# Local and coarse attention and two MoE layers in float32: the first phase's steps in another order, with fewer alternations of TensorE's kinds of work

## The chip, the cores and the metric

The kernel runs on one core of a Trainium2 chip. The metric is the device time of one execution in microseconds (us), the median of several executions.

## The reference

```python
# q, k, v: (4, 8, 576, 64)
out_d     = softmax(q_d @ k_d.T / 8) @ v_d       # q_d, k_d, v_d: means of 4 neighbours, 144 rows
out_local = softmax(where(|i - j| < 4, q @ k.T / 8, -1e9)) @ v
x = repeat(out_d, 4) + out_local                 # -> (2304, 512)
h = max(x @ w1, x @ w2, x @ w3)                  # (2304, 768)
y = h @ w_out                                    # (2304, 512)
g = max(y @ w_in, 0)                             # (2304, 2048)
out = (g * g) @ w_out2                           # (2304, 512)
```

Attention inputs are float32. The weights come as 8-byte floats and are turned into float32 on the chip.

## The kernel before

**Two phases.** Phase 1 computes attention and the first MoE layer (`y`) batch by batch, and decodes the weights of both layers. Phase 2 computes the second layer in three blocks of 768 tokens; it is one long row of matrix products, and the change doesn't touch it. Every product of the two layers runs as three products of high and low parts (`mm3`, L188 to L191: hi*hi, hi*lo, lo*hi).

**Steps and tokens.** Phase 1 is a list of some 1,300 tokens in `CFG["phase1"]`. A loop (L933) reads it, `act_on` (L679) calls the function of each token, and `manual_schedule` keeps that order on every engine. Nothing is reordered afterwards: on each engine (and in SyncE's queue of DMA issues) the instructions stand exactly in the order of the tokens, each waiting for its own inputs. So the list is at once the order of TensorE, VectorE, ScalarE, GpSimd and SyncE. The digits of a token are its batch, head pair, tile and so on; `F` and `B` are the first 256 and the last 320 positions of a batch.

- Attention, `a..`: `al`, `am`, `aN` load q, k and v (SyncE). `aq`, `ak` pool q and k (VectorE in batch 0, GpSimd after). `as` scores (TensorE, L348 and L355), `aa` maxima (VectorE), `ae` exponentials (ScalarE), `ar` sums (VectorE), `au`, `av` norms (GpSimd in batch 0, VectorE after), `at`, `af`, `aT` transposes (TensorE, L423 and L433), `ay`, `az`, `aY` copies of them, `ao` products with v (TensorE, L473 and L482), `aX`, `ah`, `ad` the sum and its high and low part (`ad` is `x_lo`, VectorE L517).
- First layer: `gg` (and `gK` in four pieces) is a gate product, 12 matmuls of 256 or 320 columns; `gM` the maximum over three gates (VectorE L591, or a copy on ScalarE for the first), `gA`, `gB` its high and low part, `gG` the output product, 18 matmuls, `gZ` its copy and store.
- Weights of the first layer come in pairs of 1 MB: `wD` load, `wR` rebias (VectorE L172), `wL` low bits (ScalarE), `wJ`, `wI` two joins (VectorE L546), `wH` high part (ScalarE), `wS` low part (VectorE L562, GpSimd for the last three pairs). Three raw buffers (`stg`) serve them, so a load waits for the `wS` three pairs back. Second layer: `x..`, `y..`, `z..` in the same manner.
- `bN` issues N products of zeros (`keep_busy`, L644) on TensorE, two matmuls each, whose results nobody reads.

**What TensorE does in phase 1.** Gates, output products, transposes and dummies use all 128 rows and columns of the array. Scores use 64 by 64 quarters of it, and products with v 70 or 72 rows by 64 columns. These two kinds are called the small kinds below, the others the full kinds. All attention steps share four PSUM banks (a second-half scores step takes two), gates and outputs four others.

Of the kernel before, what the change touches and what calls it, by code (L numbers as in the profile page):

```python
# [59 lines left out]
wR6 gg0130 gM0031 aX10F gB011 ah10F wJ6 aN11F gg0032 gM0130 wD10 ad10F wI6 gg0131 wL8 gM0032 wH6 wR8 gg0050 gM0131  # L60
gA003 wS6 gg0132 gM0050 wJ8 wD11 wL10 gg0140 wR10 gB003 gM0132 gA013 wJ10 gg0040 gM0140 wI8 gg0141 gM0040 wI10 wH8
wR11 wL11 gg0041 gB013 gM0141 wH10 wS8 gg0142 wJ11 xD4f gg0042 gM0041 gM0142 wS10 gA014 gg0051 gM0042 gA004 as11F
gM0051 wI11 gg0052 am12 xL4f aa11F gB004 gg0150 gB014 wH11 gM0052 xR4f ae11F as11B wS11 gg0151 aa11B al13 gA005
gM0150 gB005 ar11F as12F ae11B xJ4f gG000 aa12F av11F ae12F aq13 ar11B gg0152 gM0151 av11B gZ000 au11B at11F au11F
ao10B ar12F ay11F ak13 aT11F gM0152 gG001 aN11B aU10B aw12 aY11F aX10B gA015 av12F ah10B xI4f ao11F ad10B gZ001
au12F xs4 at11B xa4 aN12F as12B aU11F ay11B gB015 xc4 gG002 al20 aa12B aX11F ae12B gG003 ya4 yc4 za4 gZ002 aT11B
af11B as13F ar12B aY11B au12B az11B av12B ah11F at12F gZ003 ao11B aa13F aq20 zc4 aT12F gG010 aU11B ay12F aY12F ae13F
ad11F ak20 aX11B ah11B ar13F ao12F aN12B ad11B gZ010 av13F at12B am13 au13F aU12F at13F aX12F af12B gG013 ay12B
aN13F ah12F az12B xD4o ay13F ad12F aw13 aT13F as13B gZ013 aY13F aT12B aa13B al21 gG012 aY12B ae13B xR4o am20 ao13F
gG011 aN20F gZ012 ar13B aq21 xL4o au13B av13B aU13F aX13F ao12B gZ011 xJ4o as20F ah13F aN13B aU12B ad13F at13B aa20F  # L70
ak21 af13B gg1000 az13B aw20 ay13B ae20F gg1030 aX12B xI4o aT13B ah12B ar20F gM1000 gg1001 xe4 ad12B av20F au20F
aY13B gg1031 xD5f gM1001 gM1030 ye4 ao13B gM1031 gg1032 aU13B aX13B ah13B ze4 gg1002 gM1032 ad13B gA103 gB103 as20B
gM1002 xL5f xR5f gg1050 gA100 aa20B aN20B am21 as21F gM1050 gB100 ae20B xJ5f at20F al22 gg1040 ay20F aa21F gg1051
gM1040 aw21 ar20B ae21F av20B aT20F gg1052 gM1051 au20B xI5f aY20F at20B ao20F aq22 gM1052 xa5 ay20B aT20B aN21F
ar21F af20B aU20F gg1041 gA105 ya5 aY20B az20B aX20F za5 gg1110 ah20F gB105 gM1041 ad20F av21F xs5 gg1042 gM1110
am22 au21F xc5 as21B gM1042 ak22 gA104 gg1100 aa21B al23 gB104 gg1111 ae21B yc5 zc5 gg1101 gM1111 gM1100 ar21B aq23
av21B gg1112 gM1101 au21B xD5o as22F ak23 gM1112 gA111 gg1120 aa22F gB111 ae22F gg1140 gM1120 gg1102 ar22F gM1140
av22F au22F xL5o xR5o at21F gM1102 gg1020 ay21F gA110 xJ5o aT21F gg1021 gM1020 aY21F gB110 xI5o as22B gM1021 xe5
gg1121 aa22B al30 ye5 gg1130 ae22B xD6f gM1121 gg1122 gM1130 ar22B aq30 av22B gg1131 gM1122 ze5 au22B gA112 gg1141
gB112 ak30 gM1131 xL6f xR6f gg1132 gM1141 xJ6f gg1142 gM1132 xI6f gA113 as23F gB113 xa6 gM1142 gg1022 xs6 gA114  # L80
ao21F gB114 xc6 gM1022 gg1150 aa23F aN22F gA102 aU21F aX21F ae23F gB102 at22F ya6 gg1151 ay22F za6 ah21F gM1150
ar23F ad21F aT22F au23F gg1152 gM1151 aY22F av23F yc6 as30F gM1152 xD6o ao20B gA115 aa30F gg1010 aU20B aw22 aX20B
ae30F gB115 at21B gG110 ay21B aN21B ah20B ar30F gM1010 zc6 av30F ad20B au30F xL6o xR6o af21B gg1011 az21B gZ110 xJ6o
aT21B gg1012 am23 gM1011 aY21B xI6o ao21B gM1012 xe6 ao22F aN22B aU21B gA101 ye6 at22B xD7f aU22F at23F gG112 aw23
ay22B aX22F ay23F ah22F gB101 ad22F gG111 aN23F gZ112 aX21B ze6 ah21B ad21B xL7f xR7f af22B gG102 gZ111 xJ7f az22B
am30 xI7f aT23F gG100 gZ102 xs7 xa7 aY23F ya7 xc7 aT22B gG103 za7 aY22B yc7 gZ100 ao22B gZ103 xD7o ao23F aU22B aw30
aX22B gG101 aU23F ah22B ad22B aX23F as23B gZ101 aN23B ah23F am31 gG113 aa23B al31 xL7o ad23F xR7o ae23B gg2000 xJ7o
aN30F zc7 xI7o as30B gM2000 gZ113 ar23B aq31 gg2010 aa30B xe7 gg2020 al32 gM2010 au23B ae30B av23B ye7 gg2011 ak31
ze7 gM2020 at23B ar30B gg2012 gM2011 ay23B au30B av30B af23B aT23B az23B aq32 gM2012 as31F aY23B gA201 xD0f as31B
# [1096 lines left out]
```

## Time and profile before

| what | us |
|---|---|
| median of 3 runs (lowest, highest) | 819.86 (817.78, 820.36) |
| the profiled execution's own time | 818.96 |
| its span, first to last instruction | 817.2 |
| TensorE busy | 805.1 |
| VectorE, ScalarE, GpSimd busy | 514.3, 321.3, 173.7 |

Phase 1 lasts until 433.23 us, where the first product of phase 2 starts. The difference of 1.8 us between span and time lies around the program. Matmuls are pipelined: one starts before the last one's end is drawn, so costs are read from start to start, not from the lengths.

### The profile page before, as it was taken

How to read it: one execution, taken by the hardware profiler on the slowest of the kernel's cores; microseconds unless marked ns; L12 is line 12 of the kernel's file. 1: busy time of each engine (PE TensorE's matmuls, PEld its weight loads, DVE VectorE, ACT ScalarE, POOL GpSimd, SP SyncE). 2: the span in 40 equal slices, each digit the busy share in tenths (PEclk: the TensorE clock that was granted, in tenths of full speed). 3: DMA queues.
4: the chain of work that ended last, by engine and by line, in shares of the span. 5: the costliest groups of instructions: out<-in, count | busy, mean ns of one | idle time of the engine just before them, and what ended most of it. 6: DMA issues, size and time to landing. Idle time of an engine off the chain costs nothing.

```text
span 817.2 us, 15421 instructions
## 1 busy us (share of the span) xinstructions
PE 805.1 (99%) x6130; PEld 748.2 (92%) x6130; DVE 514.3 (63%) x960; ACT 321.3 (39%) x893; POOL 173.7 (21%) x195
## 2 busy tenths in 40 slices
...
GB/s 291 262 99 199 162 112 241 190 147 166 158 254 303 208 8 8 78 102 23 252 389 252 144 276 191 0 1 102 310 118 190 1 1 54 256 141 164 31 1 77
DMA packets 60768, 121.84 MB, mean 149 GB/s; under 512 B 5304, under 2 KB 29464, under 8 KB 60696
## 3 DMA queue, kind: packets, MB, share of 16 engines
...
q8 instruction: 48, 0.79, 0.4%
q14 instruction: 24, 0.20, 0.1%
...
## 4 chain that ended last, share of the span: by engine, by line
PE 90%; DVE 6%; DMA 2%; ACT 0%; issue 0%; SPq 0%; ACTq 0%; DVEq 0%
PE g L189 10%; PE g L191 9%; PE g L190 9%; PE po L190 8%; PE po L189 8%; PE po L191 8%; PE P L189 7%; PE P L191 7%; PE P L190 7%; PE yp L189 3%; PE yp L190 3%; PE yp L191 3%; DMA raw_p<-in_wg 1%; DVE raw_p L546 1%; DMA v<-in_vP 1%; DMA out_y<-ob 0%
## 5 line engine op out<-in xcount | busy, mean ns | idle before, releaser
L189 PE MATMUL g<-xhi,hi_p 128*128 128x256 f32 (+1 forms) x576 | 174.9, 304 | 0.0
L191 PE MATMUL g<-xhi,lo_p 128*128 128x256 f32 (+1 forms) x576 | 170.3, 296 | 1.4 <-DVE lo_p L562 1.4
L190 PE MATMUL g<-xlo,hi_p 128*128 128x256 f32 (+1 forms) x576 | 169.8, 295 | 0.0
L191 PEld LDWEIGHTS g<-xhi,lo_p 128*128 128x128 f32 x576 | 108.2, 188 | 2.0 <-DVE lo_p L562 2.0
L189 PEld LDWEIGHTS g<-xhi,hi_p 128*128 128x128 f32 x576 | 108.3, 188 | 1.8
L190 PEld LDWEIGHTS g<-xlo,hi_p 128*128 128x128 f32 x576 | 108.7, 189 | 0.0
L591 DVE TENSOR_TENSOR c<-g,c 128x320 f32<-128x320 f32 (+1 forms) x96 | 43.0, 451 | 37.9 <-PE g L191 30.1
L189 PE MATMUL yp<-hh,hi_p 128*128 128x256 f32 (+1 forms) x192 | 58.6, 305 | 0.0
L191 PE MATMUL yp<-hh,lo_p 128*128 128x256 f32 (+1 forms) x192 | 56.8, 296 | 0.0
L190 PE MATMUL yp<-hl,hi_p 128*128 128x256 f32 (+1 forms) x192 | 56.8, 296 | 0.0
L1033 DVE TENSOR_TENSOR c<-P,u 128x384 f32<-128x384 f32 x46 | 25.6, 556 | 32.4 <-PE P L191 32.4
L598 ACT ACTIVATE hh<-c 128x256 fp32r<-128x256 f32 (+1 forms) x48 | 21.0, 441 | 56.5 <-DVE c L591 56.5
L1047 DVE SCALAR_TENSOR_TENSOR c<-c 128x384 f32<-128x384 f32 x72 | 41.7, 580 | 1.7
L1045 DVE TENSOR_TENSOR c<-c 128x384 f32<-128x384 f32 x23 | 12.9, 560 | 47.3 <-ACT c L1040 47.3
L322 POOL TENSOR_TENSOR v<-v 72x256 f32<-72x256 f32 x32 | 29.3, 915 | 43.7 <-DMA v<-in_vP 43.7
L1040 ACT ACTIVATE c<-P 128x384 f32<-128x384 f32 x23 | 11.3, 491 | 65.3 <-PE P L191 65.3
L189 PEld LDWEIGHTS yp<-hh,hi_p 128*128 128x128 f32 x192 | 36.3, 189 | 0.6
L190 PEld LDWEIGHTS yp<-hl,hi_p 128*128 128x128 f32 x192 | 36.4, 190 | 0.0
L191 PEld LDWEIGHTS yp<-hh,lo_p 128*128 128x128 f32 x192 | 36.4, 189 | 0.0
L323 POOL TENSOR_TENSOR vd<-v 72x128 f32<-72x128 f32 x32 | 18.0, 561 | 80.6 <-PE o30B L473 52.0
L546 DVE SCALAR_TENSOR_TENSOR raw_p<-raw_p 128x1024 uint32<-128x1024 uint32 x24 | 34.0, 1428 | 0.0
L1029 ACT ACTIVATE p<-P 128x384 f32<-128x384 f32 x23 | 11.3, 490 | 51.4 <-PE P L191 51.4
...
## 6 DMA issues: line engine op xcount, KB each, us to landing
...
```

The source lines that it names most:

```text
L189: nc.tensor.matmul(ps, whi, xhi, start=first, stop=False, skip_group_check=more)
L190: nc.tensor.matmul(ps, whi, xlo, start=False, stop=False, skip_group_check=more)
L191: nc.tensor.matmul(ps, wlo, xhi, start=False, stop=last, skip_group_check=more)
L322: nc.gpsimd.tensor_tensor(out=v4[:, c, 0:2], in0=v4[:, c, 0:2], in1=v4[:, c, 2:4], op=ALU.add)
L323: nc.gpsimd.tensor_tensor(out=vd[:, c], in0=v4[:, c, 0], in1=v4[:, c, 1], op=ALU.add)
L546: nc.vector.scalar_tensor_tensor(out=low, in0=high, scalar=scalar, in1=in1, op0=op0, op1=ALU.bitwise_or)
L591: nc.vector.tensor_tensor(out=c_t[b, h, f], in0=ps[:, 0:N], in1=c_t[b, h, f], op=ALU.max)
L598: nc.scalar.activation(out=hhi, in_=c_t[b, h, f], func=AF.Copy)
L1029: A.activation(out=got["p1"], in_=ps["P1"][:, 0:TH], func=AF.Copy)
L1033: V.tensor_tensor(out=got[out], in0=p, in1=b, op=op)
L1045: V.tensor_tensor(out=c, in0=c, in1=c, op=ALU.mult)
L1047: V.scalar_tensor_tensor(out=c, in0=c, scalar=0.0, in1=c, op0=ALU.max, op1=ALU.mult)
```

## The change

One string changes. It holds the same tokens in another order, but for the dummies: `b21 b3 b6 b6 b3 b7 b3 b4` (53) become `b12 b13 b1 b12 b4 b5` (47). No function, tile, tile size or buffer count is touched. Counted over TensorE's steps of the whole list:

| | before | after |
|---|---|---|
| steps that are not dummies | 329 | 329 |
| changes from a full kind into a small kind | 52 | 31 |
| changes from a small kind into a gate or output | 31 | 20 |
| changes from a small kind into transposes / dummies | 15 / 6 | 10 / 1 |
| scores directly behind scores | 3 | 9 |
| products with v directly behind products with v | 2 | 7 |
| changes between scores and products with v | 7 | 17 |
| changes from gate or output to transposes / back | 37 / 38 | 40 / 44 |

The diff, cut to the start of the list up to batch 1's first transposes, and its end (`@` marks the end of attention):

```diff
--- before.py
+++ after.py
@@ -42,74 +42,73 @@
     "wlo": "vp",
     "qlo": "vp",
     "phase1": """
-b21 c0 al00 c1 am00 al01 aq00 am01 ak00 aw00 as00F n0F al02 as00B aq01 aa00F aw01 wD0 b3 ak01 ae00F aa00B as01F aq02
-b6 ae00B ar00F aa01F av00F wD1 au00F ak02 at00F ae01F aT00F ar00B as02F av00B wR0 ay00F at00B aY00F ar01F au00B
-af00B wL0 n2F aa02F ao00F av01F am02 ay00B au01F wJ0 ae02F b6 al03 wR1 ah00F wI0 at01F az00B wL1 aT00B n1F aT01F wD2
-b3 ar02F aw02 ay01F ad00F aY01F wJ1 as01B aY00B aq03 au02F av02F ao01F ak03 aa01B am03 as03F ah01F n9 wI1 ae01B b7
-aa03F n3F n1B ad01F aw03 wH1 n2B ar01B at02F as02B wR2 n0B ay02F al10 wS1 ae03F b3 aa02B av01B wH0 n3B aT02F ao00B
-ar03F aN10F aY02F aN10B wL2 wS0 b4 am10 aU00B ae02B gK00 aX00B wD9 au03F gK10 wJ2 gK01 gK02 gK11 av03F gK12 ah00B
-ar02B ao02F au01B ad00B wI2 wD3 at01B ah02F at03F ay01B af01B ad02F av02B ay03F aT03F aT01B au02B az01B wH2 as03B
-wR9 aY03F aq10 aY01B wS2 wL9 ao03F al11 aa03B gK20 aw10 ah03F gK22 wL3 wD4 gK21 ad03F ao01B wR3 ae03B gK32 wJ9 gK30
-gK31 gg0010 wJ3 aU01B gM0000 ak10 ar03B gM0001 at02B gM0010 au03B aX01B gg0011 ay02B gM0002 av03B ah01B gA000 ad01B
-wL4 af02B aT02B wI3 gg0012 az02B aY02B wR4 wH3 ao02B gM0011 gM0012 gB000 gA001 at03B aU02B wS3 aT03B ay03B af03B
-aY03B aX02B gB001 gg0020 az03B ah02B wJ4 ao03B ad02B gM0020 wI4 gg0021 aU03B aX03B wH4 wI9 as10F ah03B as10B wS4
-ad03B gg0022 al12 gM0021 o aa10B wH9 aq11 gg0100 wS9 aa10F ae10B gg0120 gM0022 wD5 ae10F ar10B gg0101 au10B av10B
-gA002 ar10F gM0100 aq12 gg0121 gM0120 gM0101 ak11 au10F wD7 av10F gg0102 gM0121 wL5 wR5 gg0122 gM0102 gA010 wJ5 wD6
-gg0110 gB010 gM0122 gA012 wI5 wL7 at10F gg0111 wR7 gM0110 wH5 ay10F gB012 am11 wJ7 at10B gg0112 ak12 ay10B wL6 gB002
-gM0111 af10B aT10F wI7 aT10B az10B aY10F gg0030 aY10B wS5 wH7 ao10F aw11 gM0112 gM0030 wD8 gg0031 gA011 wS7 aU10F
...
-gg3112 za0 gM3142 yc0 gA314 gB314 gg3040 xe0 gM3112 gA311 gg3030 xa1 ye0 xD1o gM3040 gg3041 gM3030 gB311 gg3031
-gM3041 ya1 ze0 gg3042 gM3031 gg3032 xL1o xR1o gM3042 gA304 xJ1o gg3130 xD2f gM3032 gB304 gA303 xI1o gg3050 xc1 gB303
-gM3130 gg3131 yc1 gM3050 za1 gg3051 gM3131 xL2f xR2f gg3132 xD2o gM3051 xJ2f gg3052 xI2f xe1 gM3132 gg3150 ye1
-gM3052 gA313 zc1 gA305 gB305 gg3151 gB313 gM3150 xs2 xa2 xL2o gG302 xR2o zc0 gM3151 ya2 xc2 xJ2o gG301 gZ302 yc2
-xI2o gg3152 gZ301 gG303 gM3152 xe2 ze1 gA315 ye2 gG300 gZ303 gB315 za2 gG312 gZ300 ze2 gG313 gZ312 gG310 gZ313 zc2
-gG311 gZ310 gZ311
+b12 al00 aq00 c0 ak00 al01 c1 as00F aq01 am00 as00B ak01 al02 aa00F aw00 as01F aa00B ae00F am01 b13 aa01F al03 ae00B
+ar00F aw01 aq02 av00F ak02 n2F au00F aq03 ae01F at00F am02 ar00B as02F ak03 n0F av00B ay00F aT00F ar01F wD0 as03F
+aa02F aY00F av01F au01F ao00F ae02F aa03F aw02 au00B am03 ae03F ar02F at01F at00B wD1 b1 wR0 wL0 aT01F ar03F av02F
+b12 aw03 aY01F ay00B wJ0 ay01F n1F ah00F n9 wL1 ad00F au02F wI0 ao01F n3F wR1 wD2 aT00B ah01F at02F wJ1 wH0 af00B b4
+aY00B ad01F az00B wS0 ay02F aT02F n0B aY02F as01B n1B wI1 wL2 n2B n3B wR2 ao02F wH1 al10 aa01B av03F ao00B ah02F wS1
+ae01B gK00 wD3 gK01 wJ2 gK10 gK11 gK02 ad02F au03F aU00B gK12 ar01B at03F aX00B aq10 gK20 wD4 ay03F aT03F wI2 gK22
+ah00B as02B aY03F wL3 wR3 ad00B wH2 ao03F av01B aa02B aN10B wL4 aN10F au01B at01B al11 gK21 ah03F wS2 b5 ae02B ad03F
+am10 wJ3 gK32 gK31 ay01B gK30 wD5 af01B wR4 aT01B gM0000 az01B as03B wI3 aY01B aw10 gM0001 wH3 ar02B ao01B gM0002
+ak10 aa03B gA000 av02B gg0010 wL5 au02B aU01B wS3 ae03B at02B gg0011 wJ4 gg0020 ay02B aX01B gB000 ar03B gM0010 wD6
+ah01B gM0011 af02B aT02B av03B gM0020 gg0012 az02B aY02B wI4 ao02B ad01B wH4 au03B gM0012 gg0021 wR6 wL6 wS4 gA001
+at03B aU02B wJ6 af03B aT03B ay03B gg0022 az03B aY03B aX02B gB001 gM0021 wD7 ah02B ao03B gM0022 ad02B gA002 as10B wR5
+aU03B aX03B gB002 as10F ah03B wJ5 wL7 gg0030 wR7 ad03B wJ7 al12 gM0030 gg0100 o wI5 gg0110 wI6 gM0100 wH5 wI7 wH6
+gg0101 wS5 gM0110 wH7 gg0111 wS6 gM0101 aa10F gg0102 wD8 aq11 gM0111 ae10F aa10B gg0112 aq12 wD9 gM0102 ae10B gg0120
+ar10F ak11 gM0112 au10F wR8 av10F gg0031 wS7 am11 gA011 gA010 wL9 wR9 at10F gg0032 gB011 gM0031 wL8 ar10B ay10F aw11
+wD10 aT10F gM0120 gg0121 av10B aY10F gM0032 wJ9 gA003 at10B gg0122 gB003 gM0121 ay10B wL10 wI9 af10B as11F az10B
+gB010 gM0122 wH9 ao10F aa11F gg0140 gA012 aU10F aX10F ae11F wJ8 aN11F gg0040 au10B ah10F wI8 gM0140 gg0141 gM0040
+ad10F wH8 ar11F gB012 gg0041 au11F gM0141 av11F wS8 gg0142 gM0041 wS9 am12 gg0042 gM0142 wD11 gA014 gg0130 wR10
+gB014 gM0042 gA004 wJ10 gg0150 gM0130 xD4f gB004 wL11 wR11 gg0131 gM0150 wI10 wJ11 aT10B wH10 gg0132 xR4f aY10B wI11
...
+gg3042 gM3120 gg3022 gM3042 gA304 gg3101 gB304 gM3022 yhA11 y1 gA302 yhA12 ylA11 gg3121 xa0 gB302 gM3101 y2 gg3102
+gM3121 ya0 y3 gg3122 gM3102 yhS2 gg3110 gA310 y4 gM3122 gB310 gA312 za0 gg3010 ylS2 gM3110 gB312 ylA12 gg3111 xc0
+gM3010 gg3011 yc0 gM3111 gg3030 gM3011 gg3012 gM3030 gg3140 xD1o gM3012 gA301 gB301 gg3112 gM3140 zc0 gg3141 xL1o
+xR1o gM3112 xe0 xJ1o gg3031 gA311 gM3141 ye0 xa1 gg3142 gM3031 xI1o gg3032 gB311 gM3142 gA314 gg3150 gM3032 gB314
+gA303 ya1 gg3130 gM3150 gB303 xD2f gg3151 xc1 gM3130 ze0 gg3131 yc1 gM3151 xL2f xR2f gg3152 gM3131 gG301 xJ2f za1
+gM3152 xI2f gA315 gG303 gZ301 gB315 zc1 xs2 gg3132 gZ303 gG300 gM3132 xe1 xD2o gA313 ye1 xa2 gG302 gZ300 gB313 xc2
+gG313 xL2o xR2o yc2 gZ302 ze1 gG311 xJ2o gZ313 gG312 xI2o gZ311 ya2 xe2 zc2 gG310 gZ312 ye2 za2 gZ310 ze2
 """,
 }
```

## Rows read from the trace of the kernel before

**Rows 1.** Stages of the run: window, length, busy time per engine (instructions), granted clock, DMA.

```profile
0.00:16.45 16.45, 15.01 (x149) 13.87 (x151) 8.43 (x24) 6.71 (x32) 6.07 (x15) 1.00 0.92 297
16.45:64.61 48.16, 45.29 (x588) 39.75 (x584) 46.20 (x76) 36.74 (x117) 34.60 (x38) 1.00 0.60 178
64.61:433.23 368.62, 366.12 (x3531) 355.34 (x3529) 260.69 (x505) 178.87 (x557) 125.26 (x138) 1.00 0.50 170
```

**Rows 2.** TensorE's longest wait in total: us, times, longest one.

```profile
PE g L191 <- DVE lo_p L562: 1.4, 2, 0.9
```

**Rows 3.** Timeline of TensorE around one scores step between gates: start, length, what.

```profile
308.40 0.28 PE L190 MATMUL g<-xlo,hi_p 128*128 128x256 f32 x1
308.51 0.28 PE L191 MATMUL g<-xhi,lo_p 128*128 128x256 f32 x1
308.72 0.46 PE L348 MATMUL s32F<-qkd 64*64 64x144 f32 x4
...
309.60 0.41 PE L189 MATMUL g<-xhi,hi_p 128*128 128x320 f32 x1
309.85 0.30 PE L190 MATMUL g<-xlo,hi_p 128*128 128x320 f32 x1
```

**Rows 4.** The same around four transposes between gates.

```profile
317.00 0.31 PE L191 MATMUL g<-xhi,lo_p 128*128 128x320 f32 x1
317.14 0.60 PE L423 MATMUL t32F<-const,sm32F 128*70 128x128 f32 x4
317.50 0.39 PE L189 MATMUL g<-xhi,hi_p 128*128 128x320 f32 x1
317.73 0.31 PE L190 MATMUL g<-xlo,hi_p 128*128 128x320 f32 x1
```

**Rows 5.** The same: a lone second-half scores step, then three joined steps.

```profile
162.16 0.71 PE L348 MATMUL sd20B<-qkd 64*64 64x144 f32 x8
...
163.41 0.39 PE L189 MATMUL g<-xhi,hi_p 128*128 128x256 f32 x1
...
262.21 0.46 PE L348 MATMUL s31F<-qkd 64*64 64x144 f32 x4
...
263.00 0.66 PE L348 MATMUL sd31B<-qkd 64*64 64x144 f32 x8
...
264.20 0.80 PE L482 MATMUL o23B<-pt23B,vw23B 70*64 70x64 f32 x20
...
265.21 0.39 PE L189 MATMUL g<-xhi,hi_p 128*128 128x256 f32 x1
265.43 0.28 PE L190 MATMUL g<-xlo,hi_p 128*128 128x256 f32 x1
```

**Rows 6.** The same: dummy products, the first and a later group.

```profile
1.05 7.55 PE L648 MATMUL spare<-zeros 128*128 128x128 f32 x42 [1.05 <-DVE zeros L210]
...
27.85 1.72 PE L648 MATMUL spare<-zeros 128*128 128x128 f32 x14
29.41 0.60 PE L423 MATMUL t02F<-const,sm02F 128*70 128x128 f32 x4
```

**Rows 7.** VectorE, the last `x_lo` of batch 0; TensorE, the first gate that reads it.

```profile
63.18 0.48 DVE L517 TENSOR_TENSOR xlo<-x3203B,xhi 128x320 fp32r<-128x320 f32 x1
...
64.61 0.31 PE L189 MATMUL g<-xhi,hi_p 128*128 128x320 f32 x1
```

**Rows 8.** Instructions on the tile `raw_p`: count, min/median/max in ns.

```profile
L546 DVE SCALAR_TENSOR_TENSOR raw_p<-raw_p x24: 1206/1244/2000, 19.5 to 105.8; 128x1024 uint32<-128x1024 uint32 x24
L172 DVE TENSOR_SCALAR raw_p<-raw_p x12: 683/740/1377, 16.4 to 100.6; 128x1024 f32<-128x1024 f32 x12
...
L562 DVE TENSOR_TENSOR lo_p<-raw_p,hi_p x9: 1184/1216/1790, 31.2 to 101.6; 128x1024 fp32r<-128x1024 f32 x9
```

**Rows 9.** SyncE issues one pair of weights; the stretch five us later.

```profile
43.56 0.38 SPq L531 DMA_DIRECT2D raw_p<-in_wg  x1
...
48.50:49.50 1.00, 1.00 (x11) 1.00 (x10) 1.00 (x1) 0.33 (x2) 0.92 (x2) 1.00 0.00 0
```

More of the change, by code (lines that the diff above doesn't have):

```diff
@@ L60 @@
[L60 to L89, printed above, removed]
@@ new lines @@
+aa13F ah12F ao11B aa13B ae13F gG001 aw13 ad12F xR4o aU11B ae13B aN12B ar13F at12B aX11B aN13F gG012 ay12B al21 xJ4o
+gZ001 ah11B av13F au13F aT12B am20 aq21 ar13B gZ012 at13F au13B af12B aT13F ad11B aY12B gG010 ay13F az12B aY13F xI4o
+av13B xe4 ao13F ak21 gZ010 ao12B ye4 aU13F as20F aU12B aX13F aw20 xD5f at13B ah13F aa20F gG011 ay13B ae20F aN20F
+ad13F aN13B aT13B aX12B gZ011 gg1000 xR5f ze4 ar20F ah12B av20F aY13B ad12B gg1020 xL5f au20F gM1000 gg1001 xJ5f
+gM1020 am21 xI5f af13B at20F az13B gg1010 ay20F xa5 gM1001 xs5 aT20F gg1011 gM1010 aY20F ya5 xc5 gg1002 gM1011 yc5
@@ new lines @@
+gg1012 za5 gM1002 ao20F gA100 gM1012 ao13B gB100 gA101 aU20F gB101 as20B aX20F aU13B aw21 xD5o ah20F as21F ad20F
+aa20B gg1030 aN20B aX13B gg1021 ae20B aa21F aN21F al22 gg1031 xR5o gM1021 gM1030 aq22 ae21F ar20B gg1022 am22 gM1031
+au20B zc5 av20B gg1032 ah13B gM1022 xL5o ar21F ak22 at20B gA102 ad13B gg1040 au21F gB102 av21F ay20B aT20B xJ5o
+gM1040 af20B gg1041 aY20B az20B gM1032 at21F xI5o gA103 gg1100 gM1041 xe5 ay21F gB103 aT21F gg1042 gM1100 ye5 aY21F
+ao21F gM1042 xD6f as22F gA104 aU21F gB104 as21B aX21F aa22F ah21F gg1101 aN22F aa21B ze5 ae22F gg1050 xR6f ae21B
@@ new lines @@
+gM1101 ar22F gg1110 ad21F av22F au22F al30 xL6f at22F ar21B gg1111 av21B gM1110 ay22F aq30 gM1050 xJ6f aT22F gg1112
+aY22F gM1111 xI6f gg1051 gM1112 xa6 xs6 gg1102 gA111 ak30 gM1051 xc6 ya6 gg1052 gM1102 gg1120 yc6 gA110 za6 gB110
+gM1052 as22B gM1120 gB111 gA105 au21B as30F gB105 aa22B gg1121 xD6o aa30F ae22B gg1140 gM1121 al23 xR6o gg1122 ae30F
+ar22B au22B av22B zc6 aq23 gg1141 xL6o gM1122 ar30F av30F gA112 xJ6o gM1140 gg1130 gM1141 au30F gg1150 gB112 gM1130
+xI6o ak23 gg1131 xe6 gM1150 ye6 gg1151 gM1131 xD7f gg1132 gM1151 gg1152 gM1132 ze6 gA113 xR7f xL7f gB113 as23F
```

44 lines of the change are left out of this document (27 added, 17 removed).

## The prediction

> **What bounds the kernel now.** First the stages. TensorE is busy almost through; phase 1 is 433.2 us of the 817.2 us span, and the change lies in it alone, so the remaining 384 us stay. Up to 64.61 us VectorE is nearly as full as TensorE (46.2 of 48.2 us from 16.45 on), afterwards it has room on average (260.7 of 368.6) [rows 1]. Then TensorE's waits: the longest total is 1.4 us, in two waits for the low part of a weight pair [rows 2]. So it is TensorE's own row of steps that sets the end, with VectorE close behind in the first 65 us. The clock granted to TensorE reads 1.00, its upper level of 2.4 GHz, in every stage.
>
> A busy TensorE may still lose time, so the next view is its timeline, read from start to start. Gate matmuls of 256 columns follow each other by 0.11 to 0.12 us [rows 3], of 320 by 0.15 [rows 4]. Ahead of scores the last gate matmul takes 0.21 (308.51 to 308.72), and the first gate behind the scores 0.25 instead of 0.15 (309.60 to 309.85) [rows 3]. So a visit to a small kind costs 0.09 going in and 0.10 coming out.
>
> Transposes cost nothing of the sort. Four of them take 0.36 from start to start of what follows (317.14 to 317.50), and the gate's first matmul is 0.08 longer (0.23). A full matmul of 128 columns is worth 0.11 [rows 6], so four are worth 0.44: the 0.08 that the gate loses is what the transposes gained [rows 4].
>
> **The change, part by part.** The steps are the same and their lengths too, so only alternations, dummies and waits differ. The counts are those of the change's table.
>
> Entries: 21 fewer (52 to 31) by 0.09: 1.9 us. Exits to a gate or output: 11 fewer by 0.10: 1.1 us. Exits to transposes and dummies: 10 fewer; no row prices them, so between nothing and the 0.10 of a gate, 0 to 1.0 us. I take 0.2, since transposes behind gates cost nothing either.
>
> Same kind joined: a first-half scores step lasts 0.88 to 0.89 alone [rows 3] and 0.79 ahead of another (262.21 to 263.00). A second-half one lasts 1.25 alone (162.16 to 163.41) and 1.20 behind another (263.00 to 264.20) [rows 5]. Together 0.15. Six more joined scores: 0.9 us. For five more joined products with v there is no clean row; by the scores' 0.15 it is 0.75, by bounds 0 and twice that.
>
> Scores beside products with v: 17 instead of 7. The 1.20 of the joined second half [rows 5] stays what it is though products with v follow, and the gate after them pays its usual 0.10 (265.21 to 265.43, 0.22 for 0.12). So I charge nothing for these ten. The Trainium skill (TensorEngine Tiling (Array Packing), Tiling Modes) states that changing the tiling mode drains the engine, and scores (64 rows) and products with v (70 rows) are two modes; by that rule the ten would cost like ten entries, an estimate of 0.9 us, and the gain would be 5.2 where the rows give 6.1. The row at 264.20 speaks against the charge.
>
> Dummies: six fewer, each two matmuls; 14 of them take 1.56 (27.85 to 29.41) [rows 6], so 0.22 each: 1.3 us. They fill time in which nothing else is ready, so this counts only if real work comes sooner. Bound: 0 to 1.3. Transposes between gates: more often, at nothing, as above.
>
> Sum on TensorE: 1.9 + 1.1 + 0.2 + 0.9 + 0.75 + 1.3 = 6.1 us. By my count over both lists 2.0 of it lie ahead of the first gate of batch 0's second half (`gg0100`), 4.1 behind.
>
> What is given back: that gate needs the last `x_lo` of batch 0 (`ad03B`), on VectorE. Before, `x_lo` starts at 63.18 and lasts under half a us; the gate starts at 64.61 [rows 7]. In the new list VectorE's queue ahead of `ad03B` loses the pair of `w_out` (`wR9`, `wJ9`, `wI9`) and gains `wR5`, `wJ5`, `wR6`, `wJ6`, `wR7` and two gate maxima. With the medians 0.74 for a rebias and 1.24 for a join [rows 8], and under 0.5 for a maximum, which is of the size of the `x_lo` in [rows 7]: 2.2 + 2.5 + 0.9 - 0.7 - 2.5 = 2.4 us more. So `x_lo` would end near 66.0, the gate start near 66.1. TensorE has one more gate ahead (1.6 us) and 2.0 us less of the rest, so it would be there at 64.2. That is 1.9 us of new waiting, and everything behind the gate in TensorE's queue waits with it.
>
> Some of that comes back. The first scores are no longer behind 42 dummy matmuls (7.55 us [rows 6]) but behind 24, so VectorE's maxima start sooner; it idles 8.0 of the first 16.45 us [rows 1]. Against it, 3.7 MB instead of 2.2 stand in SyncE's queue ahead of the first pair of weights, which at 297 GB/s [rows 1] is 5 us; the list puts 13 us of other VectorE work ahead of its rebias, which covers it. I take 0.3 us, bounds 0 and the whole 1.9. Given back: 1.6. Gain: 6.1 - 1.6 = 4.5 us.
>
> Moved loads: SyncE now issues pairs 5, 6, 7 ahead of `al12`, which has to wait for batch 1's scores. Pairs 6 and 7 follow `wS3` and `wS4` by about 5.2 and 5.5 us of other VectorE steps (each `wS` frees the buffer). Of a pair issued at 43.56 no traffic is left from 48.50 on, so a load takes at most 4.9 us [rows 9]. So it is just covered; if not, VectorE stands and the gate above is later by as much. ScalarE's order moves along at nothing: it has a quarter of its time free even in the full stage (36.7 of 48.2). GpSimd gets some 9 us of `w_in` and `w_out2` low parts later, ahead of phase 2, hidden behind 21 us of TensorE steps; without that cover the third quad would wait, 30 us on. VectorE's last joins have 15 us of output products over them.
>
> Later waits of TensorE I leave as they were, with 2.5 us either way as the bound, not quite twice the longest total [rows 2].
>
> Against the profiled execution: 818.96 - 4.5 = 814.5. The median stands 0.9 above that execution, so 815.4 is the prediction.
>
> **The rivals.** *TensorE keeps it all:* `x_lo` is in time because scores start sooner. For it speaks VectorE's idle start; against it, its 96% after 16.45. 819.86 - 6.1 = 813.8.
>
> *Waits take what the alternations gave:* the change does what it says, but TensorE reaches each step sooner and waits there, as it does for `lo_p` [rows 2]. Joined steps need two halves ready at once, and four shared banks free. For it speaks the first 65 us; against it the 108 us of free VectorE after them. It gives 819.9, within 2.5.
>
> *Slower, one mechanism:* ahead of the norm that batch 1's first second-half transposes need (`av10B`), VectorE's new queue holds 13 steps of pairs 5 to 8 that stood behind it: 4 rebias, 6 joins, 3 low parts. At the medians that is 4 x 0.74 + 6 x 1.24 + 3 x 1.22 = 14.1 us, which just fits: by my count at these prices VectorE has 17.3 us of steps between `ad03B` and `av10B`, TensorE 17.6 between `gg0100` and `at10B`. At the longest, 4 x 1.38 + 6 x 2.00 + 3 x 1.79 = 22.9 [rows 8]: 8.8 more, and TensorE waits at `at10B`. It decides from a stretch of 4.5 us on; at its full price 815.4 + 8.8 = 824.2. For it speaks that GpSimd is busy in most of this stage; against it, medians lie near the shortest. The Trainium skill (GPSIMD Engine Reference, Specifications) says that GpSimd shares its SBUF interfaces with VectorE and contends with instructions of two SBUF inputs, which joins and low parts are; no row here shows which instruction it was that stretched them.
>
> **How the numbers follow.** A measurement of this kernel can tell about 0.3%, 2.5 us, from no change. Forecast (gain 2.5 to 5.5) 0.45, all kept 0.25, eaten 0.20, slower 0.10. The first two are faster: 0.70. The range goes from all kept with 2.2 us of the old waits gone, 811.6, to eaten, 819.6; beyond lie the slower case and the ends of the others.
>
> **What would show it.** Entries of 0.09 and exits of 0.10 unchanged, 31 and 20 of them; joined products with v shorter by 0.15 a pair; scores of head pair 0 before 7 us; `gg0100` near 66 us, with VectorE's `x_lo` just ahead of it; phase 1 ending near 428.7; phase 2 still 384 us. I am wrong if TensorE's waits in phase 1 grow by over 4 us, if changes between scores and products with v cost 0.09 each, or if phase 2 moves.

## The result, and the profile after

The new order is slower: 827.85 us median (826.94 to 829.13) against 820.11 (817.78 to 820.49) on the same chip, a ratio of 1.0085 [1.0062, 1.0108]. The forecast was 815.4. The profiled execution has a span of 825.9 us; its phase 1 ends at 441.51 instead of 433.23 us and phase 2 lasts 384.4 us against 384.0. So 8.3 of the 8.7 us between the two profiled spans lie in phase 1. Ratios, here and below, leave out a few executions that took far longer (870 to 4,455 us) and that the medians count, so a ratio can differ a little from that of the two medians.

The stages of the new kernel (columns: window, length, busy time of TensorE, its weight loads, VectorE, ScalarE, GpSimd with their instructions, granted clock, DMA share, GB/s), cut at the first rebias of a weight pair (21.85) and at the gate `gg0100` (73.89), as [rows 1] were:

```profile
0.00:21.85 21.85, 18.06 (x209) 15.84 (x210) 13.41 (x38) 11.60 (x59) 11.18 (x23) 1.00 0.92 264
21.85:73.89 52.04, 45.03 (x523) 40.45 (x523) 41.17 (x63) 33.74 (x91) 24.94 (x28) 0.90 0.65 187
73.89:441.51 367.62, 361.77 (x3518) 353.33 (x3517) 265.05 (x504) 176.90 (x555) 133.62 (x138) 1.00 0.48 155
```

In the middle stage TensorE is busy 45.0 of 52.0 us, where it was 45.3 of 48.2 [rows 1], and the granted clock is 0.90 instead of 1.00. TensorE's longest waits (total, times, longest), to be set against [rows 2]:

```profile
PE t02B L422 <- POOL sm02B L411: 3.5, 1, 3.5
PE o01F L481 <- DMA vw<-in_vP: 3.3, 1, 3.3
PE t12F L422 <- ACT sm12B L396: 1.9, 1, 1.9
PE t00F L422 <- POOL sm00F L411: 1.6, 1, 1.6
PE t10F L422 <- DVE sm10F L411: 1.4, 1, 1.4
```

Before, the longest total was 1.4 us. Now there are waits for a load, for GpSimd, for ScalarE and for VectorE. The gate matmuls, in contrast, cost what they did. TensorE's timeline around scores and products with v in the new order:

```profile
128.66 0.28 PE L190 MATMUL yp<-hh,lo_p 128*128 128x256 f32 x1
128.87 0.46 PE L347 MATMUL s12F<-qkd 64*64 64x144 f32 x4
...
129.75 0.80 PE L481 MATMUL o10B<-pt10B,vw10B 70*64 70x64 f32 x20
130.38 0.45 PE L472 MATMUL o10B<-ptd10B,vd 72*64 72x80 f32 x8
130.76 0.71 PE L347 MATMUL sd12B<-qkd 64*64 64x144 f32 x8
```

The last matmul ahead of the scores takes 0.21 (0.12 for one of its size): the entry of 0.09. The scores take 0.88 (128.87 to 129.75), the same 0.88 as alone between gates [rows 3], though products with v follow.

To see where the time went I priced every step of both lists by its form and its neighbours, with the prices of the prediction. The old list adds up to 420.8 us, the new one to 414.7: the 6.1 us of the sum. What the traces have beyond these prices is TensorE waiting or running at half clock:

| beyond the prices, us | 0 to 36 | 36 to 64 | 64 to 146 | 146 to 200 | 200 to the end of phase 1 | sum |
|---|---|---|---|---|---|---|
| before | 6.7 | 2.0 | 1.5 | -0.1 | 1.2 | 11.3 |
| after | 12.2 | 6.2 | 5.5 | -0.1 | 1.8 | 25.7 |

So 6.1 were saved and 14.4 given back: 9.7 ahead of 64 us and 4.0 from there to 146. In this second stretch VectorE is the full engine. One row of 64 to 140 us each, of the kernel before and of the one after:

```profile
64.00:140.00 76.00, 74.78 (x722) 71.80 (x721) 70.15 (x124) 45.26 (x140) 47.40 (x43) 1.00 0.53 178
```

```profile
64.00:140.00 76.00, 71.44 (x723) 68.76 (x722) 73.58 (x114) 44.62 (x130) 47.26 (x44) 1.00 0.46 152
```

VectorE goes from 70.2 to 73.6 of 76 us, TensorE from 74.8 down to 71.4: the two have changed places. And the gate that the prediction looked at (first VectorE's `x_lo`, then the gate, as in [rows 7]):

```profile
73.35 0.86 DVE L516 TENSOR_TENSOR xlo<-x3203B,xhi 128x320 fp32r<-128x320 f32 x1
...
73.89 0.31 PE L188 MATMUL g<-xhi,hi_p 128*128 128x320 f32 x1
...
75.37 0.31 PE L189 MATMUL g<-xlo,hi_p 128*128 128x320 f32 x1
```

`x_lo` starts at 73.35, not just under 66. But TensorE doesn't wait for it: a gate reads the four head pairs one after the other, and its first matmul on this last `x_lo` is the one at 75.37, 1.2 us after `x_lo` is done. The gate itself follows the one before it without a gap, so TensorE came late by its own waits further ahead. VectorE's busy time up to there, by one row of each kernel:

```profile
0.00:63.18 63.18, 58.88 (x720) 52.32 (x720) 53.23 (x95) 43.29 (x147) 39.47 (x51) 1.00 0.69 211
```

```profile
0.00:73.35 73.35, 62.55 (x726) 55.75 (x727) 54.04 (x99) 45.34 (x149) 35.61 (x51) 0.93 0.73 210
```

It worked 54.0 us instead of 53.2, but stood still for 19.3 instead of 10.0, 5.4 of it for TensorE's gates (before 0.6) and 3.8 for weight pairs (before 0.3). The two engines wait for each other: TensorE for the results of the softmax steps of VectorE and GpSimd, VectorE's next steps for TensorE's gates. And the loads of the weights come later, since more attention loads stand ahead of them in SyncE's queue. VectorE stands still ahead of the rebias of each of the first three pairs:

```profile
21.85 0.70 DVE L171 TENSOR_SCALAR raw_p<-raw_p 128x1024 f32<-128x1024 f32 x1 [1.40 <-DMA raw_p<-in_wg]
27.71 0.73 DVE L171 TENSOR_SCALAR raw_p<-raw_p 128x1024 f32<-128x1024 f32 x1 [1.13 <-DMA raw_p<-in_wg]
34.84 0.70 DVE L171 TENSOR_SCALAR raw_p<-raw_p 128x1024 f32<-128x1024 f32 x1 [1.28 <-DMA raw_p<-in_wg]
```

Before, it does so for the first pair alone:

```profile
16.45 1.15 DVE L172 TENSOR_SCALAR raw_p<-raw_p 128x1024 f32<-128x1024 f32 x1 [0.32 <-DMA raw_p<-in_wg]
```

### The profile page after: what moved, and what is told of

It is laid out like the page before. It is cut to its first block, busy times and chain, and to the rows that moved or that the text cites. A ratio compares the mean times of both kernels' runs of the same rounds, so it can differ in the third digit from the quotient of the medians.

```text
span 825.9 us, 15399 instructions
## 1 busy us (share of the span) xinstructions
PE 803.5 (97%) x6118; PEld 748.9 (91%) x6118; DVE 518.6 (63%) x960; ACT 321.3 (39%) x893; POOL 177.6 (22%) x195
## 4 chain that ended last, share of the span: by engine, by line
PE 80%; DMA 8%; DVE 8%; POOL 1%; issue 1%; ACT 1%; SPq 0%; DVEq 0%; ACTq 0%; POOLq 0%
PE po L189 8%; PE po L188 8%; PE po L190 8%; PE P L188 7%; PE P L190 7%; PE P L189 7%; PE g L188 7%; PE g L189 7%; PE g L190 7%; PE yp L188 2%; DMA vw<-in_vP 2%; PE yp L189 2%; PE yp L190 2%; DVE raw_p L545 2%; DMA s7o<-cut_e 1%; DMA v<-in_vP 1%
## 5 line engine op out<-in xcount | busy, mean ns | idle before, releaser
L1039 ACT ACTIVATE c<-P 128x384 f32<-128x384 f32 x23 | 11.3, 491 | 65.0 <-PE P L190 65.0
L321 POOL TENSOR_TENSOR v<-v 72x256 f32<-72x256 f32 x32 | 26.5, 830 | 46.4 <-DMA v<-in_vP 40.0
L545 DVE SCALAR_TENSOR_TENSOR raw_p<-raw_p 128x1024 uint32<-128x1024 uint32 x24 | 36.0, 1514 | 0.7 <-ACT raw_p L177 0.7
L322 POOL TENSOR_TENSOR vd<-v 72x128 f32<-72x128 f32 x32 | 21.7, 679 | 64.4 <-PE o30B L472 28.0
L588 ACT ACTIVATE c<-g 128x256 f32<-128x256 f32 (+1 forms) x48 | 19.0, 404 | 36.4 <-PE g L190 36.4
```

What stands on the lines that cost most here:

```text
L321: nc.gpsimd.tensor_tensor(out=v4[:, c, 0:2], in0=v4[:, c, 0:2], in1=v4[:, c, 2:4], op=ALU.add)
L322: nc.gpsimd.tensor_tensor(out=vd[:, c], in0=v4[:, c, 0], in1=v4[:, c, 1], op=ALU.add)
L545: nc.vector.scalar_tensor_tensor(out=low, in0=high, scalar=scalar, in1=in1, op0=op0, op1=ALU.bitwise_or)
L588: nc.scalar.activation(out=c_t[b, h, f], in_=ps[:, 0:N], func=AF.Copy)
```

## The experiments

All were timed beside the kernel before on the same chip. Executions of one kernel differ by some us, mostly in the first 40 us, where the loads come in; the profiled one is one of them. The twelve traces that begin with the old order reach the first gate piece (`gK00`) between 34.1 and 39.5 us, so the first column of the table above says little by itself.

| run | median, us | before | ratio and interval |
|---|---|---|---|
| load earlier (e1) | 828.2 | 820.5 | 1.0095 [1.0067, 1.0123] |
| GpSimd steps later (e2) | 829.0 | 820.5 | 1.0110 [1.0081, 1.0139] |
| both (e3) | 828.9 | 820.5 | 1.0108 [1.0080, 1.0136] |
| both, placed better (e10) | 826.2 | 819.5 | 1.0081 [1.0054, 1.0108] |
| dummies over the wait (e16) | 827.4 | 819.6 | 1.0094 [1.0075, 1.0114] |
| old up to 152 us, then new (e5) | 825.1 | 820.5 | 1.0042 [1.0019, 1.0065] |
| old up to 146 us, then new (e12) | 823.2 | 819.5 | 1.0053 [1.0030, 1.0076] |
| old up to 34 us, then new (e13) | 825.6 | 819.6 | 1.0070 [1.0050, 1.0090] |
| the same, GpSimd steps later (e14) | 824.0 | 819.6 | 1.0059 [1.0039, 1.0079] |
| new up to 34 us, then old (e15) | 827.1 | 819.6 | 1.0097 [1.0067, 1.0126] |
| new, no joins of pairs 0 to 8 (e7) | 821.8 | 819.5 | 1.0017 [0.9995, 1.0038] |
| old, no joins of pairs 0 to 8 (e8) | 819.7 | 819.5 | 1.0005 [0.9983, 1.0026] |
| e14 without these joins (e17) | 817.0 | 820.2 | 0.9961 [0.9932, 0.9989] |
| e12, no joins of quads 4 to 7 (e18) | 814.9 | 820.2 | 0.9938 [0.9913, 0.9962] |
| old, no joins of quads 4 to 7 (e22) | 817.5 | 820.8 | 0.9963 [0.9940, 0.9985] |
| e12, quads' low parts on GpSimd (e20) | 834.5 | 820.8 | 1.0160 [1.0129, 1.0191] |
| old with the same setting (e21) | 830.0 | 820.8 | 1.0103 [1.0069, 1.0138] |
| old, nine steps joined (e19) | 821.6 | 820.2 | 1.0018 [1.0000, 1.0036] |

**First theory: two queue places.** The two long waits have a step each that seems to be at fault. SyncE issues the v windows of head pair 1 (`n1F`, at 14.50) behind two weight pairs; on GpSimd the pooling of batch 1 stands ahead of the norm that `t02B` needs. SyncE's issues in the new kernel:

```profile
11.36 0.40 SPq L530 DMA_DIRECT2D raw_p<-in_wg  x1
...
13.91 0.40 SPq L530 DMA_DIRECT2D raw_p<-in_wg  x1
14.50 0.45 SPq L257 DMA_DIRECT2D vw<-in_vP  x1
```

```diff
-ak03 n0F av00B
+ak03 n0F n1F av00B
...
-ay01F n1F ah00F
+ay01F ah00F
```

> The new order with one step moved: the load of the second head pair's v windows (n1F) stands right behind n0F, ahead of the first two pairs of weights. Theory of the queues: the 3.3 us wait of the products with v of o01F goes, and with it the stretch of half clock behind it; between o01F and the next scores (as01B) the new order lost 6.1 us against the old one, so about 822 us, and the granted clock near 30 us is 1.00. Rival, VectorE bound: the weights come 0.7 us later, VectorE sets the gates anyway, and the wait only moves to the first gates: 827 to 828. Rival, the alternations cost more than their rows show: 827 to 828 too, with no wait anywhere.

Measured: 828.2, no gain. The wait at `o01F` is gone, and two others stand further on, both followed by half clock: a new one of 2.1 us for ScalarE's `x_hi` near 45 us, and that for GpSimd's `sm02B` (2.4) at 56. The next run moves the GpSimd steps.

```diff
-aY01B aw10 gM0001
+aY01B gM0001
...
-gM0002 ak10 aa03B
+gM0002 aa03B
...
-av03B gM0020
+av03B aw10 ak10 gM0020
```

> The new order with two steps moved on GpSimd: the pooling of v and k of batch 1 (aw10, ak10) stands behind the norms of the softmax of the last two head pairs (av03B) and not ahead of them. Theory of the queues: the 3.5 us wait of the transposes t02B goes, and the half clock behind it; the new order lost 3.8 us in this place, so about 824 us, with the wait for o01F's load and its half clock near 30 us unchanged. Rival, VectorE bound: the sums of the softmax come late by themselves, t02B waits for them nearly as long, or the gain is lost at the gate that needs the last x_lo: 827 to 828.

Measured: 829.0. Again the wait moved, now to the next head pair:

```profile
PE td03B L431 <- POOL pd03B L410: 4.2, 1, 4.2
```

My edit had a share in this: `pd03B` is written by `au03B`, which I had left behind the two steps. With both edits:

> Both moves together. Theory of the queues: the two gains add, 6.1 and 3.8, so about 818 us, 2 us under the kernel before, with a granted clock of 1.00 throughout; left are the 4 us of smaller waits from 66 to 150 us. Rival, VectorE bound: 826 to 828 with the waits moved to the gates behind 64 us. If the two are one (VectorE hides what the second gives once the first is gone): 822.

Measured: 828.9, with 4.4 us at the same place. So the run was made again with `aw10 ak10` behind `au03B`:

```diff
-au03B gM0012
+au03B aw10 ak10 gM0012
```

> As the run with both moves, but the pooling of v and k of batch 1 (aw10, ak10) stands behind au03B, the last of the four norms. In the earlier one it stood between av03B and au03B, and the transposes of the last head pair waited 4.4 us for it. Theory of the queues: with that out of the way no long wait is left ahead of the gate gg0100, 821 us or less. Theory of VectorE's queue: VectorE's idle time ahead of the last x_lo falls from 20 to some 15 us and TensorE is earlier there, but from 74 to 140 us VectorE has more in front of what TensorE needs than in the old order (14.7 us more ahead of av10B), so most of it is lost again at at10F, at10B and at12F: 824 to 828.

Measured: 826.2. No wait is left at `t02B` or `td03B`. In the profiled execution (830.1, its slowest) the longest now names VectorE's `x_lo`, which reads the products with v in PSUM and stands in the queue behind rebias steps that had waited 2.1 and 0.7 us for weight pairs (the `x_hi` that it needs stands on ScalarE behind a step that had waited 2.8 us for the second of them):

```profile
PE td02F L431 <- DVE xlo L515: 3.3, 1, 3.3
PE t00F L421 <- POOL sm00F L410: 2.8, 1, 2.8
PE t12F L421 <- ACT sm12B L395: 1.9, 1, 1.9
PE t10F L421 <- DVE sm10F L410: 1.5, 1, 1.5
```

In all four runs TensorE reaches `gg1000` between 163.2 and 163.7 us, later than in the new order itself (162.56), whatever the first 64 us looked like. Mending single places does not help: the first theory falls.

**The clock.** The long waits are followed by half clock. Rows of the new kernel around the wait at `o01F`:

```profile
24.00:28.00 4.00, 1.31 (x11) 0.59 (x9) 2.80 (x4) 0.83 (x3) 3.92 (x6) 1.00 1.05 247
28.00:30.00 2.00, 1.40 (x18) 1.28 (x19) 1.53 (x2) 1.12 (x2) 0.72 (x1) 0.50 0.82 242
30.00:34.00 4.00, 4.00 (x21) 3.38 (x21) 2.92 (x4) 2.44 (x6) 0.00 (x0) 0.50 1.07 195
```

```diff
-wI0 ao01F n3F
+wI0 b16 ao01F n3F
```

> The new order with 16 more dummy products (3.4 us) right ahead of the products with v of o01F, over the time in which TensorE waits for the load of their v windows. The load comes no sooner, so only the clock can differ. If the idle wait is what lowers the clock, it stays at 1.00 until 36 us and the steps behind the wait take 2.8 us less up to the first second-half scores (as01B). The time: 825 if TensorE keeps that, 827 to 828 if VectorE's queue takes it back further on.

Measured: 827.4. The clock stays at the upper level:

```profile
28.00:30.00 2.00, 2.00 (x19) 1.64 (x20) 1.90 (x2) 0.67 (x1) 1.16 (x2) 1.00 0.98 308
30.00:34.00 4.00, 4.00 (x66) 3.69 (x61) 2.47 (x4) 2.86 (x7) 0.00 (x0) 1.00 1.10 208
```

Between 30 and 34 us TensorE does 66 instructions instead of 21, and it reaches `gK00` at 36.79 instead of 38.27. But `t02B` then waits 3.6 us, and `gg1000` starts at 162.60 against 162.56. What the clock gave came back as waiting.

**Which part of the order is at fault?** Each kernel here runs one list up to a point and then the remaining tokens in the other list's order. The joints (old tokens, then new; in the last diff the other way round):

```diff
 at13B aa20F ak21 af13B
+xI4o xe4 ye4 aw20
```

> The old order up to batch 1's first gate (gg1000, at 151.7 us), the new order behind it. Theory of the queues: the harm is done ahead of this gate, and behind it the new order keeps what its fewer alternations save, 2.9 us by the same prices less 0.7 us of waits: about 818 us. Rival, the new order's changes between scores and products with v (10 of them more in all) cost like entries or its waits grow all along: 820 or more, no gain over the kernel before.

Measured: 825.1. At this joint the lists differ in nine tokens, and the splice itself made a wait of 3.8 us (`td13B`). A joint with five differing tokens was the better question:

```diff
 ar13B aq21 xL4o au13B
+xJ4o xI4o av13B xe4
```

> The old order up to the norm av13B (about 146 us), the new order behind it; the two lists agree there but for five steps, where the earlier splice moved some ten. Theory: behind 146 us VectorE has room, and the new order keeps its 2.9 us of fewer alternations less under 1 us of waits: 817.5 to 818.5. Rival, the alternations cost more than their rows, or the order behind is at fault too: 820 or more.

Measured: 823.2, slower than before, although 2.9 us are saved by the prices. Its waits lie behind the joint, most of them on VectorE (the first two of the list are the start's):

```profile
PE td13B L431 <- DVE x3213F L497: 1.3, 1, 1.3
PE s21F L346 <- DVE x3220F L497: 1.3, 1, 1.3
...
PE t13B L421 <- DVE sm13B L410: 1.1, 1, 1.1
```

Beyond the prices there are 4.7 us between 146 and 200 us, where the new kernel itself has none. That fits with VectorE as the late one: the new kernel reaches `gg1000` at 162.56 us and this one at 156.87, so VectorE has 5.7 us less there.

```diff
 aY02F aN10B wL2 wS0 b4
+ao02F av03F ah02F gK00
```

> The old order up to am10, just ahead of the first gate pieces (gK00, near 34 us), the new order behind it. By the prices of the steps 4.3 us of the 6.1 saved lie behind this point. If the new order's harm is its start (attention loads ahead of weights, the clock's fall), the rest keeps its saving except for aw10 and ak10 ahead of av02B (up to 4 us): 816 to 820. If the rest loses by itself, since VectorE's queue and the shorter stretches of gates between dependent attention steps no longer cover the chains, it gives back at least what it saves: 820 to 825.

> The same with aw10 and ak10 behind au03B on GpSimd. Harm in the start alone: 816. The rest loses by itself: 820 to 824, with waits of TensorE at gg0100, at10F to at12F and behind 146 us.

Measured: 825.6 and 824.0. The rest of the new order loses by itself, even from the old start, though the lists differ in nine tokens at this joint too, and a part of the loss may be the joint's.

```diff
 ao00B ah02F wS1 ae01B
+ar01B as02B aa02B av01B
```

> The opposite: the new order up to gK00, the old one behind it. By gK00 the new order had waited 6.4 us more than the old one and saved 2.8 by prices (of which dummies are the largest part): 823 to 824 if this start costs what it shows. If TensorE catches up behind it, because VectorE was the later one anyway: 817 to 820.

Measured: 827.1, above the forecast. The new start alone costs as much as the whole change: in the traces TensorE is 6.6 us behind the old order at `gK00` and 7.2 at the end of phase 1. So the losses do not add up: each part of the new order alone gives back more than it saves. It fits that a part that comes late hides the waits of the next.

**VectorE's load.** If VectorE is what TensorE waits for everywhere, less work on it must make the saving visible.

```diff
-wJ0
-wI0
...
-wJ8
-wI8
```

> The new order without the two joins of pairs 0 to 8 on VectorE (18 instructions, wJ and wI), so the low bits of these weights are left out: 18 x 1.24 = 22 us less on VectorE, nothing less on TensorE. Theory now, after the first four runs: between 16 and 140 us the new order is bound by VectorE's queue, every wait of TensorE behind 36 us comes from it, and moving one load or one GpSimd step only moves the wait. Then the waits from 50 us on go with their half clock, the load's wait at o01F (3.3 us and the half clock behind it) stays: 819 to 821 us, and VectorE idles between 64 and 140 us. Rival, the place of single steps in GpSimd's and ScalarE's queues: t02B and t12F wait as before, 825 to 828. Rival, alternations cost more: 827, without waits.

> The old order without the same 18 joins. If TensorE's row of steps bounds the kernel before, the time stays within 2 us of it (its waits that name VectorE add up to some 4 us): 817 to 820. If VectorE was already the bound in its first 140 us, it gains 5 us or more.

Measured: 821.8, a little above the forecast, and 819.7. The new order gains 6 us from 22 us less on VectorE, the old one nothing that can be told. Behind 64 us the new order then has no growing lag: `gG010` starts 3.8 us sooner than in the new order, `gg2100` 5.7. All of this lies behind `gg0100`. Ahead of it VectorE has 16 us less to do, and TensorE reaches the gate at 73.82 us instead of 73.89 (rows up to there without the joins, then with them):

```profile
0.00:73.80 73.80, 64.47 (x730) 57.57 (x731) 38.35 (x88) 45.14 (x149) 30.22 (x52) 0.93 0.73 210
```

```profile
0.00:73.80 73.80, 63.00 (x730) 56.20 (x731) 54.49 (x100) 45.34 (x149) 36.06 (x51) 0.93 0.73 210
```

So in this start (by one trace each) it is not VectorE's work that holds TensorE up, and the expectation that every wait behind 36 us would go failed there: `t02B` still waits 1.9 us and a gate 1.7 for `x_hi`, and half clock follows at 58.1 to 61.5 us. `o01F`'s load and `t00F` cost it as before. The same omission on e14, whose start is the old one:

> The old start with the new order behind it and GpSimd's two steps moved (824.0 us), now without the two joins of pairs 0 to 8 on VectorE; the low bits of these weights are left out. If VectorE's queue is what takes the saving ahead of 146 us, TensorE's waits at t10F, t12F and at the gates' x_hi go and the 4.3 us of prices stay: 815 to 817 us, under the old order without the joins (819.7, its profiled run 815.6). If the cover between dependent steps is too thin whatever VectorE has to do, the waits stay: 821 to 824.

Measured: 817.0, faster than the kernel before (0.9961), and the long waits are gone. The longest in e14:

```profile
PE g L187 <- ACT xhi L511: 4.9, 1, 4.9
PE t10F L421 <- DVE sm10F L410: 2.1, 1, 2.1
PE t12F L421 <- ACT sm12B L395: 2.0, 1, 2.0
```

and without the joins:

```profile
PE spare L646 <- DVE zeros L208: 1.1, 1, 1.1
PE g L187 <- ACT xhi L511: 0.9, 1, 0.9
PE t12F L421 <- ACT sm12B L395: 0.8, 1, 0.8
```

Beyond the prices e14 has 24.3 us and e17 7.3; the old order without its joins 8.0 against 11.3. These are single traces, of e14's slowest execution (828.1) and e17's fastest (811.0); the medians are 7.0 us apart. Of the 4.3 us of prices 0.4% (3.6 us) shows between the ratios of e17 and e8, whose intervals just touch. Plainer is the stretch behind the start, which the loads of the first 40 us no longer disturb:

| from `gg0100` to the end of phase 1, us | all joins | without those of pairs 0 to 8 |
|---|---|---|
| old order (before, e8) | 368.6 | 368.0 |
| new order (after, e7) | 367.6 | 362.0 |
| old start, then new order (e14, e17) | 368.3 | 361.5 |

The new list has one gate (1.5 us) ahead of `gg0100` that the old one has behind it. Apart from that the new order is 4.5 to 5.0 us shorter without the joins, where the prices say 4.1, and 0.5 to 1.2 us longer with them. (The other traces of the new order with all joins lie between 366.5 and 370.7.) So from here on it is VectorE's work that takes the saving. The same question behind 146 us, with the second layer's quads:

```diff
-xJ4f
-xI4f
...
-xJ7o
-xI7o
```

> The old order up to 146 us and the new one behind it (823.2 us), now without the two joins of the second layer's quads 4 to 7 on VectorE (16 instructions), so that low bits of those weights are left out. In the new list these quads are decoded earlier among the attention steps of batches 1 and 2. If that VectorE work makes t13B, as21F and their neighbours wait, the waits of 152 to 172 us (4.5 us) go: 817 to 819. If it is the order of the attention steps alone: 822 to 823.

> The control for the run that left out the 16 joins of quads 4 to 7 and came to 814.9: the old order without the same joins (low bits of these weights left out). If it stays at 818 to 820.5, the 5 us between them are what the new order's fewer alternations give once VectorE does not make TensorE wait. If it falls to 816 or less, the joins cost the old order as much, and the new one has no gain of its own.

Measured: 814.9 and 817.5. Rows of 140 to 190 us of e12, e18 and the control, in this order:

```profile
140.00:190.00 50.00, 45.96 (x517) 43.84 (x518) 40.40 (x81) 26.63 (x88) 20.41 (x24) 1.00 0.69 216
```

```profile
140.00:190.00 50.00, 49.56 (x576) 47.60 (x575) 37.49 (x85) 29.09 (x100) 16.86 (x24) 1.00 0.73 238
```

```profile
140.00:190.00 50.00, 50.00 (x546) 47.68 (x545) 32.59 (x81) 27.99 (x105) 17.75 (x30) 1.00 0.59 195
```

TensorE's busy time rises from 46.0 to 49.6 us; beyond the prices 4.7 us fall to 0.8. The old order gains too (817.5), so of the 8 us between e12 and e18 about 3 are not the new order's. The ratios of e18 and e22 differ by 0.25%, 2.1 us, not far from the 2.9 us of prices, but their intervals overlap: the times alone do not show it. The traces agree with them: from `gG010` to the end of phase 1 e18 takes 296.3 us and the control 298.5.

Can VectorE be relieved with nothing left out? The low parts of quads 4 to 7 on GpSimd:

```diff
-    "qlo": "vp",
+    "qlo": "pp",
```

> The old order up to 146 us and the new one behind it (823.2 us), now with the low parts of quads 4 to 7 on GpSimd instead of VectorE (one setting); nothing is left out. That takes about 15 us off VectorE between 130 and 260 us (8 of 1.32 us and 8 of 0.6) and puts some 30 us on GpSimd, which has more than that free there. If VectorE's decoding is what makes TensorE wait behind 146 us, some 3 us or more of the 4.5 us of waits go: 817 to 820. If GpSimd's slower steps hold the weights' buffers up, or the waits depend on single joins in front of the wrong step: 822 or more.

> The control: the old order with the same setting. TensorE hardly waits for VectorE behind 146 us there (2 us in all), so 818 to 820.5 if it is bound by its own steps.

Measured: 834.5 and 830.0, and the control was expected at 818 to 820.5. GpSimd's queue also pools q and k for the next scores, and these come late now (`s13F` waits 1.4 and 1.5 us for `qkd`). The average of free time on GpSimd misled me as VectorE's had before.

**Only TensorE's steps moved.** Nine tokens of the old list go one or two TensorE steps forward or back, the other engines' orders stay, for example:

```diff
-as11F gM0051
+as11F as11B gM0051
...
-ao13F gG011
+ao13F ao12B gG011
...
-as23F gB113 xa6 gM1142 gg1022 xs6 gA114 ao21F
+as23F gB113 xa6 gM1142 ao21F gg1022 xs6 gA114
```

> The old order with nine steps of TensorE moved by one or two places, each so that a visit to a small kind joins the next one; no step of VectorE, ScalarE, GpSimd or SyncE changes its place. By the prices of entries, exits and joined steps it saves 1.7 us. If the prices are right and the cover stays, TensorE's stretch from the gate gg0100 to the end of phase 1 takes 366.9 instead of 368.6 us, and the time is 818 against 819.7 (just about what five rounds can tell). If moving even one place costs its saving in waits, no change: 819.7 or more.

Measured: 821.6. From `gg0100` (64.39) to the end of phase 1 (433.10) it takes 368.7 us, as before. The prices hold once more (419.1 instead of 420.8), and 1.7 us of new small waits take their place.

## Why the prediction was wrong

- **Held.** The prices of entries (0.09 in the median of 10 lone ones behind 66 us), exits (0.10, of 14), joined scores and joined products. For the last the guess of 0.15 a pair was right: a first-half product ahead of another takes 0.75 instead of 0.85, a second-half one behind another 0.96 instead of 1.01. Put on every step of both lists they give the sum of 6.1 again, and the trace shows the part behind `gg0100` once the joins are left out (4.5 to 5.0 us for 4.1). Phase 2 did not move.
- **Held: no charge between scores and products with v.** A first-half scores step takes 0.88 between gates (at 230.72), 0.88 ahead of a product (128.87) and 0.89 behind one (158.22). The rule of the Trainium skill that was weighed (TensorEngine Tiling (Array Packing), Tiling Modes) would have taken 0.9 of the 6.1; no such charge shows here.
- **Failed: "Later waits of TensorE I leave as they were, with 2.5 us either way".** Beyond the prices the trace grew by 14.4 us, well over the 4 us that the prediction named as its sign of being wrong: 9.7 ahead of 64 us, 4.0 from there to 146, 0.7 behind. For the waits behind 64 us the step rested on the sentence that VectorE "has room on average (260.7 of 368.6)". That average spans 369 us; in the 76 us behind 64 the old order had VectorE busy for 70.2, and the room lies later. E7 and e17 show it: without 18 joins on VectorE the new order keeps its saving from `gg0100` on. E13 and e14 show that the order behind 34 us turns the gain into a loss even without the new start.
- **Failed: "Given back: 1.6".** I compared VectorE's queue at one gate and found 2.4 us more work there. The trace shows 0.8 us more work and 9.4 us more standing still, and no wait at this gate at all: TensorE reached it 9.3 us late by waits further ahead. A queue's work gives its end only if the engine never waits, and here it waited for loads and for TensorE's gates. E15 shows that this start alone loses as much as the whole change. The first scores did come sooner (5.41 instead of 8.54 us), but the transposes behind them then waited 1.6 us for GpSimd's norm (`t00F`; 1.6 to 3.5 in the eight traces of this start, 0.2 to 1.2 in those of the old).
- **Failed: moved loads that other work covers.** The first pair's load did come 5 us later, but the "13 us of other VectorE work" did not cover it: VectorE stood still for it and for the next two. The pairs that I found "just covered" were 6 and 7, by the 4.9 us of a single later load; the first two pairs took 10.5 and 13.8 us from issue to rebias. And one load I had not priced, `n1F` behind pairs 0 and 1, made a wait of 3.3 us with half clock behind it. E1 and e16 show that neither the wait nor its clock was worth anything by itself.
- **Not priced: GpSimd's order and the clock.** `aw10` and `ak10` ahead of `av02B` made the 3.5 us wait. The same holds: mended, it moved on.
- **The rivals.** "Waits take what the alternations gave" (0.20) had the right mechanism and too small a size: it stopped at the 6.1 us that were saved. The slower rival's place, `at10F` and `at10B`, shows 1.4 and 0.3 us of waits, a small part.

What stays open is the cause ahead of `gg0100`, where most was lost. In the new start it is neither VectorE's joins (e7) nor one of the three places that were mended (e1, e2, e10, e16); from the old start on, leaving the joins out did help there (e17 reaches `gg0100` 10.3 us ahead of e14, 3.9 of it already at `gK00`). Two things set every trace of the new start apart from those of the old: a longer wait at `t00F`, and a first rebias at 21.8 to 24.4 us instead of 15.2 to 18.1, since its load is issued at 11.4 to 14.3 instead of 6.9 to 8.3. No run put these loads back ahead, and none left the joins out together with the mended places of this start. Behind `gg0100` it is shown that joins left out bring the saving back; which VectorE steps would have to move is open, and a list that keeps all work and has the saving was not found.
